# Two passes of cached attention and MLP on one core: rows 0 to 4 finished in mid-run, rows 5 to 7 together at the end, and wo loaded in longer runs

## The chip, the cores and the metric

One core of a Trainium2 chip. The time is what the device takes for one execution, in microseconds (us), as the median over several runs. Before the change it is 1152.2 us. (A trace is one execution. On the packet ruler below, the two traces of the run a_quick drift apart by up to 1.5 us.)

## The reference

Two blocks, A (attention with a cache) and B (an MLP with a mixer), are applied twice in turn to eight rows of one token each.

```python
# B = 8 rows, 1 token, D = 448; 16 query heads on 8 K/V heads, 4096 positions, Dh = 256
def _A_ref(x, k_cache, v_cache, wq, wo):
    q = (x @ wq) ...                        # 8 x 16 heads x 256
    scores = einsum("bhqd,bhkd->bhqk", q, k) * (Dh ** -0.5)
    o = einsum("bhqk,bhkd->bhqd", softmax(scores), v)
    return o.reshape(B, 1, 4096) @ wo
def _B_ref(x, w1, w2, w3, w4):
    ...                                     # the mixer shifts along a sequence of length 1: x1 = x
    return x1 + gelu(layernorm(x1) @ w3) @ w4
x = x + A(layernorm(x)); x = x + B(layernorm(x))
x = x + A(layernorm(x)); x = x + B(layernorm(x))
```

K and V are 128 MB each, in bf16. Both passes read all of them. A row has 32 MB of K and V, and the kernel's pool holds 15 MB of it at one time.

## The kernel before

K and V come in blocks of 1 MB into a pool of 15 slots. An item of the program is one block, K or V, of one row in one pass. Row b's second pass follows soon after its first, so ten blocks of each row are kept on the chip between the passes. Those ten slots are taken from the first pass of a row until its second one; the other five are all that the stream of blocks has in the meantime. I call these five the ring. Slots go back to the ring in the order in which they come free, and every load is issued from one queue (SyncE).

```python
NC = 15
kept = [(GP - 1, kv, n) for n in range(4) for kv in range(2)] + [(GP - 2, 0, n) for n in (0, 2)]
...
def emit_loads(most=None):
    while loads and places and n != most:
        it = loads.pop(0)
        p = where[it] = places.pop(0)
        ...
        nc.sync.dma_start(dst[:], src)          # 1 MB, in packets of 8192 B
```

A K block is transposed in place by VectorE, multiplied by TensorE and then free; a V block is multiplied by TensorE and then free. Between the items the program slips in steps of the per-row work (generators): the row's output projection, its MLP, and q of the second pass. After the second pass there is the *finish*: output projection, MLP and store. The kernel before finishes rows 0 to 6 together, under the last row's items, and the last row alone at the very end.

```python
def rest(b, st):                                # the finish of rows 0 .. 6
    nb = Bn - 1
    yield from out_cols(lambda i: OT2[:, i % 2, i // 2, :nb], wo_sb, NB2, 0, nb, 1)
    yield from mlp(0, nb)
    ...                                         # transpose, cast to bf16
    nc.sync.dma_start(out[:nb].rearrange("b s d -> (b s) d"), xo)
...
elif done == 4 and not final:
    add_gen("last", b, last(b, st), idx + 1, idx + (7 if b == Bn - 2 else 13), 6)
    if b == Bn - 2:
        add_gen("last", 0, rest(b, st), idx + 1, len(items) - 2, 21)
if not (ps == 0 and stays(it)):                 # the item's slot is free
    if final and stays(it) and at_end is not None:
        ...                                     # two slots become scratch for the end
    else:
        places.append(p)
emit_loads()
step(idx)
```

The last row's second-pass V blocks are used as the stationary operand, so that its output comes out in columns:

```python
def pv_cols(o_ps, v, a, gp):
    for y in range(16):
        for j in range(2):
            nc.tensor.matmul(o_ps[:, j, 2 * g : 2 * g + 2],
                v[:, y * Dh + 128 * j : y * Dh + 128 * j + 128],
                ptw[:, a, 4 * (y % 4) + y // 4, 6:8], ...)
...
nc.sync.dma_start(wo_sb[:], A_wo.rearrange("(g p) d -> p g d", p=128))
```

The softmax here doesn't subtract the row's maximum and nothing guards it: scores larger than these inputs give would overflow.

Of the kernel before, what the change touches and what calls it, by code (L numbers as in the profile page):

```python
# [17 lines left out]
def kernel(  # L18
# [43 lines left out]

    kept = [(GP - 1, kv, n) for n in range(4) for kv in range(2)] + [(GP - 2, 0, n) for n in (0, 2)]
    LAG = 4

    consts = ctx.enter_context(tc.tile_pool(name="consts", bufs=1))
    work = ctx.enter_context(tc.tile_pool(name="work", bufs=2))
# [119 lines left out]
    def norm(x, nb, twice):  # L187



        def room(name, shape, at):
            n = shape[0] * shape[1]
            if nb == 1:
                t = chn.tile([128, n], FP32, tag=name)
                ap = t[:]
            else:
                ap = scratch(at, n * nb)
            return ap.rearrange("p (s f b) -> p s f b", s=shape[0], f=shape[1])

        def bc(ap):  # L200
            return ap.unsqueeze(1).to_broadcast([128, 4, nb])

        xx = room("xx", (2, 4), 0)
        nc.vector.tensor_mul(xx[:, 0], x, wv[:].unsqueeze(2).to_broadcast([128, 4, nb]))
        nc.vector.tensor_mul(xx[:, 1], xx[:, 0], x)
        xs = room("xs", (1, 2), 512)[:, 0]
        nc.vector.tensor_reduce(
            xs, xx.rearrange("p s f b -> p s b f"), mybir.AxisListType.X, ALU.add
        )
        yield  # L210
        st = ps_m.tile([128, 2, nb], FP32, tag=bank[0])
        nc.tensor.matmul(st[:], ones, xs, start=True, stop=True)
        yield
        mv = room("mv", (1, 2), 528)[:, 0]
        nc.vector.tensor_copy(mv, st[:])
        var = room("var", (1, 1), 608)[:, 0, 0]
        if nb == 1:
            nc.vector.scalar_tensor_tensor(
                var, mv[:, 0], mv[:, 0], mv[:, 1], ALU.mult, ALU.subtract, reverse1=True
            )  # L220
        else:
            nc.vector.tensor_mul(var, mv[:, 0], mv[:, 0])
            nc.vector.tensor_sub(var, mv[:, 1], var)


        ve = room("ve", (1, 2), 544)[:, 0]
        n = 2 if twice else 1
        nc.vector.tensor_scalar(ve[:, 0], var, 0.0, EPS, ALU.max, ALU.add)
        if twice:
            nc.vector.tensor_scalar(ve[:, 1], var, 0.0, EPS * EPS / (1 + EPS), ALU.max, ALU.add)  # L230
        rs = room("rs", (1, 2), 560)[:, 0]
        nc.gpsimd.tensor_tensor(  # L232
            rs[:, 0:n].rearrange("p n b -> p (n b)"),
            ve[:, 0:n].rearrange("p n b -> p (n b)"),
            nhalf[:].to_broadcast([128, n * nb]),
            ALU.pow,
        )
        xc = room("xc", (1, 4), 576)[:, 0]
        nc.vector.tensor_tensor(xc, x, bc(mv[:, 0]), ALU.subtract)
        yield  # L240
        if nb > 1:
            yield
        c = (1 + EPS) ** -0.5 if twice else 1.0
        rl = rs[:, n - 1]
        parts = ((slice(0, 128), 0, 3, 0), (slice(0, 64), 3, 4, 3), (slice(64, 128), 3, 4, 4))
        for pp, f0, f1, to in parts:
            dst = xbs(nb)[pp, to : to + f1 - f0, :]
            if nb == 1:
                nc.vector.tensor_scalar(dst, xc[pp, f0:f1], rl[pp], c, ALU.mult, ALU.mult)
            else:  # L250
                nc.vector.scalar_tensor_tensor(
                    dst,
                    xc[pp, f0:f1],
                    c,
                    rl[pp].unsqueeze(1).to_broadcast([pp.stop - pp.start, f1 - f0, nb]),
                    ALU.mult,
                    ALU.mult,
                )
        if twice and nb == 1:
            nc.vector.scalar_tensor_tensor(x, xc, rs[:, 0], x, ALU.mult, ALU.add)  # L260
        elif twice:
            nc.vector.tensor_tensor(xc, xc, bc(rs[:, 0]), ALU.mult)
            nc.vector.tensor_add(x, x, xc)
        yield
# [130 lines left out]
    def half(o_ps, zall, g8, OT):  # L395


        rz = yield from z_cols(zall, range(2 * g8, 2 * g8 + 2))

        R = chn.tile([128, 8], FP32, tag="R")  # L400
        nc.vector.tensor_mul(
            R[:].rearrange("p (g n) -> p g n", n=4),
            rz[:].rearrange("p n g -> p g n"),
            fold[:].rearrange("p (g n) -> p g n", n=4),
        )
        o_sb = chn.tile([128, Dh], FP32, tag="o_sb")
        nc.scalar.copy(o_sb[:], o_ps[:, Dh * g8 : Dh * g8 + Dh])
        yield
        ot_ps = ot_bank[:, 64 * g8 : 64 * g8 + 16].rearrange("p (j h) -> p j h", j=2)
        for j in range(2):  # L410
            nc.tensor.matmul(  # L411
                ot_ps[:, j], o_sb[:, 128 * j : 128 * j + 128], R[:], start=True, stop=True
            )
        yield
        nc.vector.tensor_copy(OT[:, :, 8 * g8 : 8 * g8 + 8], ot_ps)
        yield
# [35 lines left out]
    def first_last(b, st):  # L452

        yield from half(st["o"], st["z"], 1, OT2[:, :, :, b])
        if b == Bn - 1:
            yield from add_half(st["y"], OT2[:, :, :, b : b + 1], 1, 1, claim(st), 2)

    def claim(st):

        return st.setdefault("begun", 0) == 0 and st.update(begun=1) is None  # L460
# [3 lines left out]

    def rest(b, st):

        nb = Bn - 1
        yield from out_cols(lambda i: OT2[:, i % 2, i // 2, :nb], wo_sb, NB2, 0, nb, 1)
        yield from mlp(0, nb)
        xh = scratch(768, 2 * nb).bitcast(BF16).rearrange("p (c b) -> p c b", c=4)  # L470
# [132 lines left out]
    def pv_cols(o_ps, v, a, gp):  # L603

        g = 2 * gp + a // 2
        for y in range(16):
            for j in range(2):
                nc.tensor.matmul(  # L608
                    o_ps[:, j, 2 * g : 2 * g + 2],
                    v[:, y * Dh + 128 * j : y * Dh + 128 * j + 128],  # L610
                    ptw[:, a, 4 * (y % 4) + y // 4, 6:8],
                    start=(a % 2 == 0 and y == 0 and j == 0),
                    stop=(a % 2 == 1 and y == 15),
                    skip_group_check=True,
                )
# [6 lines left out]
    ps0 = rows_to_cols(x_row, Bn)  # L622
    nc.vector.tensor_copy(xT[:], ps0[:])
    emit_loads(5)
    nc.sync.dma_start(wo_sb[:], A_wo.rearrange("(g p) d -> p g d", p=128))
    load_split(w3_sb, B_w3, F)
    nc.sync.dma_start(w4_sb[:], B_w4.rearrange("(c p) d -> p c d", p=128))
    for _ in project_q(0, Bn, qT1[:]):
# [13 lines left out]

    def step(idx):

        for kind in ("chain", "last"):
            bank[0] = kind
            e = next((e for e in gens if e["kind"] == kind), None)
            if e is None:
# [8 lines left out]
    first_of = {}  # L657
    for idx, (n, kv, c) in enumerate(items):
        first_of.setdefault((tasks[n][:2], kv), idx)
    yF, rz_gp, at_end = None, None, False  # L660

    for idx, it in enumerate(items):
        n, kv, c = it
# [4 lines left out]
        if kv == 0:  # L668
# [11 lines left out]
            if "o" not in st:  # L680
# [1 line left out]
                st["o"], st["z"] = o_banks[0], z_t  # L682
                o_banks.append(o_banks.pop(0))
                if final:
                    st["y"] = o_banks[0][:, 0:4].unsqueeze(2)
                    oc = st["o"][:, 0 : 2 * Hq].rearrange("p (j h) -> p j h", j=2)
            if not (ps == 1 and stays(it)):
                transpose_k(slot)
# [8 lines left out]
        else:  # L697
# [6 lines left out]
            if final and gp in free:  # L704
                pv_cols(oc, slot, c, gp)
                if c % 2 == 1:
# [4 lines left out]
                    run(  # L711
                        add_cols(
                            st["y"],
                            lambda i: OT2[:, i % 2, i // 2, b : b + 1],
                            wo_sb,
                            range(h0, h0 + 4),
                            1,
                            5,
                            first=claim(st),
                            stop=(gp == free[-1] and u == 1),  # L720
# [5 lines left out]
            if c == 3:  # L726
# [5 lines left out]
                elif done == 4 and ps == 0:  # L732
                    add_gen("chain", b, chain(b, st), idx + 1, first_of[(1, b), 0] - 1, 30)
                elif done == 4 and not final:
                    add_gen("last", b, last(b, st), idx + 1, idx + (7 if b == Bn - 2 else 13), 6)
                    if b == Bn - 2:
                        add_gen("last", 0, rest(b, st), idx + 1, len(items) - 2, 21)
        if not (ps == 0 and stays(it)):
            if final and stays(it) and at_end is not None:

                if not at_end:
                    at_end, spare[:] = True, []
                spare.append(slot)
                if len(spare) == 2:
                    at_end = None
            else:
                places.append(p)
        emit_loads()
        step(idx)
    while gens:  # L750
        step(10 * len(items))
    bank[0] = "last"


    xs = xT[:, :, Bn - 1 : Bn]
    nc.vector.tensor_add(xs, xs, st["y"])
    ident2 = spare[1][:, 0:256].bitcast(FP32)
    nc.vector.tensor_copy(ident2, identb[:])
    W = D // 4
    o_row = ps_m.tile([128, W], FP32, tag="chain")  # L760
    nc.vector.memset(o_row[:], 0.0)
    HT = run(mlp_hidden(Bn - 1, 1))
    for q in range(4):
        for fc in range(4):
            w = 128 if fc < 3 else 64
            lo, hi = max(W * q, 128 * fc), min(W * q + W, 128 * fc + w)
            if lo < hi:
                nc.tensor.matmul(
                    o_row[32 * q : 32 * q + 1, lo - W * q : hi - W * q],
                    xT[:w, fc, Bn - 1 : Bn],  # L770
                    ident2[:w, lo - 128 * fc : hi - 128 * fc],
                    start=(lo == W * q),
                    stop=False,
# [2 lines left out]
    for c in range(HC):  # L776
        for q in range(4):
            nc.tensor.matmul(
                o_row[32 * q : 32 * q + 1, :],
                HT[:, c, :],  # L780
                w4_sb[:, c, W * q : W * q + W],
                start=False,
# [2 lines left out]
            )  # L785
    xo = spare[1][:, 256 : 256 + W]
    nc.vector.tensor_copy(xo, o_row[:])
    nc.sync.dma_start(
        out[Bn - 1].rearrange("s (q w) -> (s q) w", q=4),
        xo.rearrange("(q r) w -> q r w", r=32)[:, 0, :],  # L790
    )


# [28 lines left out]
```

## Time and profile before

| before | us |
|---|---|
| median of the runs | 1152.2 |
| span of the profiled run | 1149.58 |
| 5,000th packet of 8192 B down | 123.53 |
| 44,000th / 48,000th packet of 8192 B down | 896.64 / 977.66 |
| last packet of 8192 B down (all K and V is on the chip) | 1131.96 |
| last matmul on V ends | 1137.82 |

The packet times are counted from the packet records in the trace, data packets of 8192 B in the order of their ends: wq's large pieces and all K and V blocks consist of such packets, 55,680 in each kernel that keeps ten blocks. They are a ruler along the run: the same packet number means the same bytes moved.

The page cuts the span into 40 slices. These are its rows for the granted TensorE clock, the busy share of the DMA engines and the rate, and its packet count:

```profile
PEclk9999998555755557555665557555575556555655
DMA  9999999999999999999999999999999999999993
GB/s 353 375 421 420 419 398 414 420 421 396 418 421 420 420 419 419 420 402 413 419 419 420 405 417 419 420 420 399 419 420 420 410 399 414 420 419 393 412 420 143
DMA packets 69500, 465.91 MB, mean 405 GB/s; under 512 B 7127, under 2 KB 13158, under 8 KB 13670
```

The DMA engines are the bound: busy in every slice but the last, at 420 GB/s in most. What is not at 420 is lost: the first two slices, in which the weights load, one dip in each row's cycle (398, 396, 402, 405, 399, 399, 393), and the tail.

The windows view gives for a stretch its length, the busy time and instruction count of each engine, the granted clock, the DMA share and GB/s. Here are the two stretches of before in which wo loads:

```profile
core 0: us, PE busy (x) PEld busy (x) DVE busy (x) ACT busy (x) POOL busy (x), PEclk, DMA share, GB/s
25.00:30.00 5.00, 2.05 (x64) 1.66 (x64) 4.97 (x3) 1.10 (x2) 0.00 (x0) 1.00 1.06 337
30.00:35.00 5.00, 1.24 (x36) 1.00 (x36) 0.00 (x0) 0.48 (x3) 0.00 (x0) 1.00 1.09 338
```

The engines are busy all the time (share over 1) and move only 337 GB/s: wo's rows come in packets of 896 B, which take 46 ns each at the median where one of 8192 B takes 312 (packet records of before). And the same view over the end of row 5's cycle, when row 6's ten kept blocks hold their slots and five are left:

```profile
905.00:920.00 15.00, 8.00 (x198) 6.58 (x199) 8.09 (x11) 1.87 (x4) 0.00 (x0) 0.50 1.00 400
920.00:935.00 15.00, 10.79 (x268) 8.50 (x268) 9.54 (x20) 1.49 (x3) 0.70 (x1) 0.50 1.00 391
935.00:950.00 15.00, 11.48 (x304) 9.23 (x297) 7.96 (x15) 0.27 (x1) 0.55 (x1) 0.50 1.00 407
950.00:965.00 15.00, 10.29 (x314) 8.02 (x313) 3.93 (x7) 3.48 (x7) 0.00 (x0) 0.68 1.01 410
```

I call this the tight stretch. Counted from the issue times and the packet records, 1.0 to 2.2 MB are outstanding there when the next load has been issued (bytes of all loads issued before it, less the bytes of packets that have ended).

The chain of waits of before (start, duration, what) near the end of the run, in extracts:

```profile
1087.62 1.80 PE y_ps L318 x64
...
1094.61 1.80 PE y_ps L318 x32
...
1103.78 2.60 POOL slot_80 L232
...
1107.30 2.22 DVE slot_86 L546
...
1120.03 1.21 PE y_ps L318 x28
...
1136.02 1.81 PE o_111 L608 x64
```

The chain there is TensorE's, not the DMA's. `y_ps` is the seven-row finish (output projection, later w4); the POOL piece is its pow over 14 columns, behind which VectorE and then a K transpose wait. The timeline (start, duration, engine, line, what, and in brackets the idle time before it) shows the last V blocks of before and what follows:

```profile
1133.94 1.01 PE L608 MATMUL o_111<-ptw,slot_79 128*128 128x2 bf16 x32
1135.95 1.01 PE L608 MATMUL o_111<-ptw,slot_88 128*128 128x2 bf16 x32
1136.83 0.99 PE L608 MATMUL o_111<-ptw,slot_82 128*128 128x2 bf16 x32
...
1146.75 0.27 DVE L787 CAST slot_87<-o_row 128x112 bf16<-128x112 f32 x1 [1.58 <-PE o_row L778]
1147.06 0.61 SPq L788 DMA_DIRECT2D out_dram<-slot_87  x1
```

The last bytes were down at 1131.96 us, yet TensorE comes to the last block only at 1136.83: it lags.

### The profile page before, as it was taken

How to read it: one execution, taken by the hardware profiler on the slowest of the kernel's cores; microseconds unless marked ns; L12 is line 12 of the kernel's file. 1: busy time of each engine (PE TensorE's matmuls, PEld its weight loads, DVE VectorE, ACT ScalarE, POOL GpSimd, SP SyncE). 2: the span in 40 equal slices, each digit the busy share in tenths (PEclk: the TensorE clock that was granted, in tenths of full speed). 3: DMA queues.
4: the chain of work that ended last, by engine and by line, in shares of the span. 5: the costliest groups of instructions: out<-in, count | busy, mean ns of one | idle time of the engine just before them, and what ended most of it. 6: DMA issues, size and time to landing. Idle time of an engine off the chain costs nothing. (4 is left out here: it accounts for less than half of the span.)

```text
span 1149.6 us, 36516 instructions
## 1 busy us (share of the span) xinstructions
PE 677.8 (59%) x17177; PEld 522.2 (45%) x17177; DVE 554.0 (48%) x712; ACT 114.1 (10%) x234; POOL 15.6 (1%) x25
## 2 busy tenths in 40 slices
PE   3134677557645665456754576536765476547786
PEld 2023455345533554345543455425544365426666
DVE  5145454455444545455354554445544554445452
ACT  0001011100110111001110101010011001010100
POOL 0000000000000000000000000000000000000000
PEclk9999998555755557555665557555575556555655
DMA  9999999999999999999999999999999999999993
GB/s 353 375 421 420 419 398 414 420 421 396 418 421 420 420 419 419 420 402 413 419 419 420 405 417 419 420 420 399 419 420 420 410 399 414 420 419 393 412 420 143
DMA packets 69500, 465.91 MB, mean 405 GB/s; under 512 B 7127, under 2 KB 13158, under 8 KB 13670
## 3 DMA queue, kind: packets, MB, share of 16 engines
q1 hardware_dynamic: 69350, 463.58, 98.5%
q8 instruction: 134, 2.20, 0.8%
q14 instruction: 16, 0.13, 0.0%
HBM read 463.54 MB, written 0.01 MB: 403 GB/s over the span
## 5 line engine op out<-in xcount | busy, mean ns | idle before, releaser
L553 PEld LDWEIGHTS <-qbd 128*8 128x8 bf16 x8192 | 200.5, 111 | 439.7 <-issue 340.5
L594 PEld LDWEIGHTS <-ptw 128*8 128x8 bf16 x3968 | 110.2, 111 | 78.0 <-issue 29.4
L562 ACT ACTIVATE p_n<-sc_110 128x512 bf16<-128x512 f32 x32 | 42.5, 1327 | 409.0 <-PE sc_110 L553 409.0
L562 ACT ACTIVATE p_n<-sc_109 128x512 bf16<-128x512 f32 x32 | 42.5, 1327 | 382.3 <-PE sc_109 L553 382.3
L318 PEld LDWEIGHTS <-wo_sb 128*128 128x128 bf16 (+1 forms) x1600 | 64.4, 124 | 16.1 <-issue 15.3
L546 DVE STREAM_TRANSPOSE slot_79<-slot_79 128x2048 uint32<-128x2048 uint32 x19 | 43.8, 2308 | 39.0 <-DMA slot_79<-in_A_k_cache_dram 36.0
L546 DVE STREAM_TRANSPOSE slot_86<-slot_86 128x2048 uint32<-128x2048 uint32 x19 | 43.9, 2311 | 38.6 <-DMA slot_86<-in_A_k_cache_dram 36.0
L546 DVE STREAM_TRANSPOSE slot_81<-slot_81 128x2048 uint32<-128x2048 uint32 x18 | 41.6, 2309 | 37.4 <-DMA slot_81<-in_A_k_cache_dram 37.4
L318 PE MATMUL y_ps<-OT,wo_sb 128*128 128x1 bf16 (+1 forms) x1280 | 55.1, 176 | 3.0 <-issue 3.0
L546 DVE STREAM_TRANSPOSE slot_89<-slot_89 128x2048 uint32<-128x2048 uint32 x16 | 37.0, 2310 | 32.1 <-DMA slot_89<-in_A_k_cache_dram 32.0
L546 DVE STREAM_TRANSPOSE slot_88<-slot_88 128x2048 uint32<-128x2048 uint32 x15 | 34.6, 2308 | 29.8 <-DMA slot_88<-in_A_k_cache_dram 29.8
L546 DVE STREAM_TRANSPOSE slot_90<-slot_90 128x2048 uint32<-128x2048 uint32 x14 | 32.3, 2308 | 31.9 <-DMA slot_90<-in_A_k_cache_dram 31.9
L546 DVE STREAM_TRANSPOSE slot_82<-slot_82 128x2048 uint32<-128x2048 uint32 x14 | 32.3, 2307 | 29.5 <-DMA slot_82<-in_A_k_cache_dram 29.5
L546 DVE STREAM_TRANSPOSE slot_80<-slot_80 128x2048 uint32<-128x2048 uint32 x14 | 32.3, 2304 | 29.3 <-DMA slot_80<-in_A_k_cache_dram 29.3
L546 DVE STREAM_TRANSPOSE slot_84<-slot_84 128x2048 uint32<-128x2048 uint32 x12 | 27.7, 2309 | 37.5 <-DMA slot_84<-in_A_k_cache_dram 37.3
L546 DVE STREAM_TRANSPOSE slot_78<-slot_78 128x2048 uint32<-128x2048 uint32 x13 | 30.0, 2310 | 29.4 <-DMA slot_78<-in_A_k_cache_dram 29.4
L274 PEld LDWEIGHTS <-wq_sb 128*128 128x128 bf16 x1152 | 33.9, 104 | 18.2 <-issue 16.6
L546 DVE STREAM_TRANSPOSE slot_83<-slot_83 128x2048 uint32<-128x2048 uint32 x13 | 30.0, 2306 | 25.2 <-DMA slot_83<-in_A_k_cache_dram 25.2
L546 DVE STREAM_TRANSPOSE slot_92<-slot_92 128x2048 uint32<-128x2048 uint32 x12 | 27.6, 2304 | 21.8 <-DMA slot_92<-in_A_k_cache_dram 21.8
L582 ACT CAST ptw<-misc 128x128 bf16<-128x128 f32 x64 | 17.5, 273 | 203.9 <-PE misc L575 160.1
L274 PE MATMUL q_ps<-xb_126,wq_sb 128*128 128x1 bf16 x1024 | 31.8, 165 | 4.0 <-issue 2.7
L546 DVE STREAM_TRANSPOSE slot_87<-slot_87 128x2048 uint32<-128x2048 uint32 x10 | 23.1, 2311 | 20.6 <-DMA slot_87<-in_A_k_cache_dram 20.5
(217 smaller groups left out, 958.1 us busy)
## 6 DMA issues: line engine op xcount, KB each, us to landing
slot_79<-in_A_k_cache_dram SPq DMA_DIRECT2D x19, 1024.0 KB, 14.8
slot_86<-in_A_k_cache_dram SPq DMA_DIRECT2D x19, 1024.0 KB, 19.1
slot_81<-in_A_v_cache_dram SPq DMA_DIRECT2D x19, 1024.0 KB, 18.9
slot_81<-in_A_k_cache_dram SPq DMA_DIRECT2D x18, 1024.0 KB, 12.6
slot_89<-in_A_v_cache_dram SPq DMA_DIRECT2D x17, 1024.0 KB, 9.7
slot_82<-in_A_v_cache_dram SPq DMA_DIRECT2D x17, 1024.0 KB, 17.6
slot_86<-in_A_v_cache_dram SPq DMA_DIRECT2D x17, 1024.0 KB, 10.2
slot_88<-in_A_v_cache_dram SPq DMA_DIRECT2D x17, 1024.0 KB, 13.6
```

The source lines that it names most:

```text
L274: nc.tensor.matmul(q_ps[:, j * Hq + h, :], w, xbs(nb)[:, xi, :], start=(fc == 0), stop=(fc == 3),)
L318: nc.tensor.matmul(r, w[:, i, lo:hi], rhs(i), start=(first and fc == 0 and i == rows[0]), stop=(stop and i == rows[-1]), skip_group_check= ...
L546: nc.vector.transpose(w, w)
L553: nc.tensor.matmul(sc[32 * k : 32 * k + 8, 128 * x : 128 * x + 128], qbd[:, ep, gp].rearrange("p a h -> p (a h)"), kv[:, k, 2 * half + e2, ...
L562: nc.scalar.activation(p_sb[:].rearrange("p t i x -> p x t i"), sc[:].rearrange("p (x t i) -> p x t i", x=4, t=4), ACT.Exp, scale=scale_ex ...
L582: nc.scalar.copy(ptw[:, :, :, 6:8], pt_ps.rearrange("p t k (a h) -> p a (t k) h", a=4),)
L594: nc.tensor.matmul(o_ps[32 * q : 32 * q + 8, 256 * (g // 4) : 256 * (g // 4) + 256], ptw[:, a, 4 * (y % 4) + y // 4, w : w + 8], v[:, y * ...
```

## The change

Three things are meant. The finish of most rows leaves the end of the run, where it delays the last row, and goes to mid-run, where the engines beside the DMA have time (over the span of before PE is busy for 59% and VectorE for 48%). The last three rows share one finish, since their row count hardly changes the number of matmuls (for one row at the end of before 160 on wo and 56 on w3). And wo's rows are laid so that a partition holds d = 2p and 2p+1 of each head, which makes one run of 1792 B out of two of 896 B; for this V and o_sb are read with a step of two as stationary operands. The diff also splits the pow of the layernorm, one instruction for each of its variances, the one that is needed first in front. The finish in mid-run needs scratch space, and takes a slot of the ring for it until it is done. The diff, cut to its core:

```diff
+    R = Bn - 3
@@ norm
-        nc.gpsimd.tensor_tensor(rs[:, 0:n] ..., ve[:, 0:n] ..., nhalf ..., ALU.pow)
+        for i in range(n)[::-1]:
+            nc.gpsimd.tensor_tensor(rs[:, i], ve[:, i], nhalf[:].to_broadcast([128, nb]), ALU.pow)
@@ half
-                ot_ps[:, j], o_sb[:, 128 * j : 128 * j + 128], R[:], start=True, stop=True
+                ot_ps[:, j], o_sb[:, j : Dh : 2], Rz[:], start=True, stop=True
@@ first_last (the last row)
-            yield from add_half(st["y"], OT2[:, :, :, b : b + 1], 1, 1, claim(st), 2)
+            yield from add_half(st["y"], OT2[:, :, :, R:], 1, Bn - R, claim(st), 2)
@@ rest
-        nb = Bn - 1
+        nb = R
@@ pv_cols
-                    v[:, y * Dh + 128 * j : y * Dh + 128 * j + 128],
+                    v[:, y * Dh + j : y * Dh + Dh : 2],
@@ loads
-    nc.sync.dma_start(wo_sb[:], A_wo.rearrange("(g p) d -> p g d", p=128))
+    nc.sync.dma_start(
+        wo_sb[:].rearrange("p (h j) d -> p h j d", j=2),
+        A_wo.rearrange("(h p j) d -> p h j d", p=128, j=2),
+    )
@@ the item loop
-                    add_gen("last", b, last(b, st), idx + 1, idx + (7 if b == Bn - 2 else 13), 6)
-                    if b == Bn - 2:
-                        add_gen("last", 0, rest(b, st), idx + 1, len(items) - 2, 21)
+                    add_gen("last", b, last(b, st), idx + 1, idx + 13, 6)
+                    if b == R - 1:
+                        rest_from = idx + 14
...
+            elif borrow == "wanted":
+                borrow, spare[0] = p, slot
             else:
                 places.append(p)
+        if type(borrow) is int and not any(e["kind"] == "rest" for e in gens):
+            places.append(borrow)
+            borrow = None
         emit_loads()
+        if idx == rest_from:
+            borrow = "wanted"
+            add_gen("rest", 0, rest(b, st), idx + 4, idx + 60, 22)
@@ the end
-    xs = xT[:, :, Bn - 1 : Bn]
+    xs = xT[:, :, R:]
...                                             # the same with three columns
-    nc.sync.dma_start(out[Bn - 1] ...)
+    for n in range(nb):
+        (nc.sync, nc.scalar)[n % 2].dma_start(out[R + n] ...)
```

More of the change, by code (lines that the diff above doesn't have):

```diff
@@ L231, in norm @@
         rs = room("rs", (1, 2), 560)[:, 0]
-        nc.gpsimd.tensor_tensor(
-            rs[:, 0:n].rearrange("p n b -> p (n b)"),
-            ve[:, 0:n].rearrange("p n b -> p (n b)"),
-            nhalf[:].to_broadcast([128, n * nb]),
-            ALU.pow,
-        )
+        for i in range(n)[::-1]:
+            nc.gpsimd.tensor_tensor(rs[:, i], ve[:, i], nhalf[:].to_broadcast([128, nb]), ALU.pow)
         xc = room("xc", (1, 4), 576)[:, 0]
@@ L240, in norm @@
         yield
-        if nb > 1:
+        if nb > 3:
             yield
@@ L398, in half @@
         rz = yield from z_cols(zall, range(2 * g8, 2 * g8 + 2))
-        R = chn.tile([128, 8], FP32, tag="R")
+        Rz = chn.tile([128, 8], FP32, tag="Rz")
         nc.vector.tensor_mul(
-            R[:].rearrange("p (g n) -> p g n", n=4),
+            Rz[:].rearrange("p (g n) -> p g n", n=4),
             rz[:].rearrange("p n g -> p g n"),
@@ L643, in step @@
     def step(idx):
-        for kind in ("chain", "last"):
+        for kind in ("chain", "last", "rest"):
             bank[0] = kind
@@ L659 @@
         first_of.setdefault((tasks[n][:2], kv), idx)
-    yF, rz_gp, at_end = None, None, False
+    rz_gp, rest_from, borrow, ends = None, None, None, []
     for idx, it in enumerate(items):
@@ L684 @@
                 if final:
-                    st["y"] = o_banks[0][:, 0:4].unsqueeze(2)
+                    st["y"] = o_banks[0][:, 0 : 4 * (Bn - R)].rearrange("p (f b) -> p f b", f=4)
                     oc = st["o"][:, 0 : 2 * Hq].rearrange("p (j h) -> p j h", j=2)
@@ L713 @@
                             st["y"],
-                            lambda i: OT2[:, i % 2, i // 2, b : b + 1],
+                            lambda i: OT2[:, i % 2, i // 2, R:],
                             wo_sb,
                             range(h0, h0 + 4),
-                            1,
+                            Bn - R,
                             5,
@@ L734 @@
                 elif done == 4 and not final:
-                    add_gen("last", b, last(b, st), idx + 1, idx + (7 if b == Bn - 2 else 13), 6)
-                    if b == Bn - 2:
-                        add_gen("last", 0, rest(b, st), idx + 1, len(items) - 2, 21)
+                    add_gen("last", b, last(b, st), idx + 1, idx + 13, 6)
+                    if b == R - 1:
+                        rest_from = idx + 14
         if not (ps == 0 and stays(it)):
-            if final and stays(it) and at_end is not None:
-                if not at_end:
-                    at_end, spare[:] = True, []
-                spare.append(slot)
-                if len(spare) == 2:
-                    at_end = None
+            if final and stays(it) and len(ends) < 2:
+                ends.append(slot)
+                if len(ends) == 2:
+                    spare[:] = ends
+            elif borrow == "wanted":
+                borrow, spare[0] = p, slot
             else:
                 places.append(p)
+        if type(borrow) is int and not any(e["kind"] == "rest" for e in gens):
+            places.append(borrow)
+            borrow = None
         emit_loads()
+        if idx == rest_from:
+            borrow = "wanted"
+            add_gen("rest", 0, rest(b, st), idx + 4, idx + 60, 22)
         step(idx)
@@ L751 @@
         step(10 * len(items))
-    bank[0] = "last"
-    xs = xT[:, :, Bn - 1 : Bn]
+    bank[0] = "rest"
+    nb = Bn - R
+    xs = xT[:, :, R:]
     nc.vector.tensor_add(xs, xs, st["y"])
@@ L761 @@
     nc.vector.memset(o_row[:], 0.0)
-    HT = run(mlp_hidden(Bn - 1, 1))
+    HT = run(mlp_hidden(R, nb))
     for q in range(4):
@@ L768 @@
                 nc.tensor.matmul(
-                    o_row[32 * q : 32 * q + 1, lo - W * q : hi - W * q],
-                    xT[:w, fc, Bn - 1 : Bn],
+                    o_row[32 * q : 32 * q + nb, lo - W * q : hi - W * q],
+                    xT[:w, fc, R:],
                     ident2[:w, lo - 128 * fc : hi - 128 * fc],
@@ L778 @@
             nc.tensor.matmul(
-                o_row[32 * q : 32 * q + 1, :],
+                o_row[32 * q : 32 * q + nb, :],
                 HT[:, c, :],
@@ L787 @@
     nc.vector.tensor_copy(xo, o_row[:])
-    nc.sync.dma_start(
-        out[Bn - 1].rearrange("s (q w) -> (s q) w", q=4),
-        xo.rearrange("(q r) w -> q r w", r=32)[:, 0, :],
-    )
+    for n in range(nb):
+        (nc.sync, nc.scalar)[n % 2].dma_start(
+            out[R + n].rearrange("s (q w) -> q (s w)", q=4),
+            xo.rearrange("(q r) w -> q r w", r=32)[:, n],
+        )
 _INS = ['A_x', 'A_k_cache', 'A_v_cache', 'A_wq', 'A_wo', 'B_x', 'B_w1', 'B_w2', 'B_w3', 'B_w4']
```

## The prediction

> **What bounds it now.** The DMA engines. The page's slice row shows DMA at 9 in all but the last slice, mostly 420 GB/s; 466 MB at that rate are about 1,109 of 1,149.6 us. By five-microsecond windows the rest is a 3 us start, about 5 us lost while weights load (337 GB/s between 25 and 35 us, with wo), some 12 us in dips to 360-390 GB/s late in each row's cycle, and a tail without DMA. In the timeline the last V block's bytes are down near 1,132 us, but it is used up only at 1,137.8; the last row's MLP and store end at 1,149.6.
>
> The tail lags because TensorE, at a granted clock near 0.5, is nearly the whole chain of waits from 1,087 us on. It holds the seven-row finish: out projection (160 matmuls, 4.6 us), w3 (1.8), w4 (2.9), transpose (0.5), and 2.6 us in which VectorE, and K transposes behind it, wait for GpSimd's 14-column pow.
>
> **Terms, estimates from those durations.**
>
> 1. wo in 1792 B runs. Its 4,096 packets of 896 B take 46 ns each (8192 B: 312; 3584 B: 144); a line through these gives 79 ns for 1792 B, the few in the trace took 88. [...] 11.8 us become 10.1 to 11.3; DMA-bound, so it counts: -1.2 us.
>
> 2. The seven-row finish leaves the tail. Without its 10 us of TensorE work and the pow wait, the last V block is done about 2 us after landing instead of 6: -3.7 us.
>
> 3. The three-row finish is wider. Matmul counts are equal; the first pow has 3 columns (one 0.55 us, two 0.70, so 0.85), variance takes one more VectorE instruction (0.2), gelu 42 columns, the third store follows the first on its queue (0.6): +1.1 us on the final chain.
>
> 4. The five-row finish borrows one of five free ring slots (ten of fifteen hold kept K/V) for some 50 items, just over row 5's tight stretch (908 to 957 us now). There 1.0 to 1.6 MB are outstanding before each issue, and a slot is held about 4 us after landing. With four slots, and the finish's own work, the DMA will sometimes run dry; today this stretch loses 2 us of 45, I expect 4 to 5. Lost DMA time is not regained: +2.3 us (0 to 6).
>
> 5. Stride-2 weight loads of V and o_sb: no cost. [...] the trace's stride-2 selector loads take about 26 ns apart, but none is 128 columns wide.
>
> Sum -1.5; I lean slightly lower. All 8192 B traffic stays, so 2% is very unlikely.
>
> **Predicted: 1150 us, range 1145 to 1155. Faster by over 2%: 0.02; within 2%: 0.96; slower: 0.02.**
>
> **What would show it.** 1: more GB/s from 25 to 37 us, the first V block used 1 us earlier. 2: no seven-column matmuls late; the last V block used within 2 us of landing. 3: from the last V matmul to the end about 13 us, now 11.8. 4: a deeper GB/s dip at 905 to 960 us with less outstanding, and in no other row. 5: 32 of the last row's V weight loads still in 0.95 us.
>
> **What would make it wrong.** Four slots starving the DMA much more (1153 and up) or not at all (1147); slower strided weight loads (up to 1 us per V block at the end); TensorE still lagging in the last row from instruction stalls; dearer output stores.

-1.2, -3.7, +1.1, +2.3 and nothing for term 5 make the -1.5. Term 5 rests on the selector loads alone (15 of them take 0.42 us at 171.86 us of before), and for loads of 128 columns it was my estimate. The instruction stalls and dearer stores named at its end are possibilities, not findings.

## The result and the profile after

After: 1152.53 us median (1151.27 to 1153.37, four runs); before beside it 1152.24. The ratio is 1.0002 with a 95% interval of 0.9984 to 1.0019: the same. (A ratio here is the mean time of one kernel's fast runs over that of the other's fast runs of the same rounds, so it is not quite the ratio of the medians.)

Nothing gained, but not because nothing happened. The traces on the common ruler:

| us | before | after | difference |
|---|---|---|---|
| 5,000th packet of 8192 B down | 123.53 | 122.51 | -1.02 |
| 44,000th | 896.64 | 895.57 | -1.07 |
| 44,000th to 48,000th (row 5's tight stretch) | 81.02 | 85.31 | +4.29 |
| 48,000th to the last | 154.30 | 154.82 | +0.52 |
| last packet to the end of the last matmul on V | 5.86 | 1.50 | -4.36 |
| from there to the end of the span | 11.76 | 12.80 | +1.04 |
| span | 1149.58 | 1150.00 | +0.42 |

From the page after, the rate by slices and the packets:

```profile
GB/s 356 387 421 418 421 397 419 420 419 397 419 419 420 417 419 420 420 401 413 419 419 420 407 415 419 421 419 399 420 419 419 391 372 397 420 421 395 400 420 191
DMA packets 67464, 465.91 MB, mean 405 GB/s; under 512 B 7141, under 2 KB 11122, under 8 KB 11634
```

The second slice rose from 375 to 387 (wo), and slices 32 to 34 fell from 410, 399, 414 to 391, 372, 397: the dip of one row's cycle is deeper, and of no other row by as much. Some 2,000 packets fewer are wo's. The windows view after, first where wo loads, then over the tight stretch:

```profile
25.00:30.00 5.00, 2.05 (x64) 1.66 (x64) 5.00 (x3) 0.94 (x1) 0.00 (x0) 1.00 1.02 374
30.00:35.00 5.00, 1.24 (x36) 1.00 (x36) 0.13 (x1) 0.64 (x3) 0.00 (x0) 1.00 1.06 384
...
905.00:920.00 15.00, 8.65 (x211) 7.14 (x211) 9.01 (x16) 1.92 (x5) 0.00 (x0) 0.50 0.92 364
920.00:935.00 15.00, 12.09 (x307) 9.88 (x310) 8.84 (x20) 1.49 (x3) 1.07 (x2) 0.50 0.98 373
935.00:950.00 15.00, 12.50 (x322) 10.30 (x315) 7.50 (x17) 0.27 (x1) 0.54 (x1) 0.50 0.97 367
```

337 became 374 and 384 GB/s. In the tight stretch 400, 391 and 407 became 364, 373 and 367, and the DMA share fell to 0.92: the engines ran out of work. By the same count as before, 0.4 to 1.5 MB are outstanding when a load is issued there, more often than not under 0.8. In before, just before the stretch, up to 890 us, it is nearly 6 MB.

The chain of waits after, from 1082 us on:

```profile
1082.23 14.22 DMA slot<-in_A_v_cache_dram
...
1096.53 19.75 DMA slot<-in_A_v_cache_dram
...
1116.36 19.78 DMA slot<-in_A_v_cache_dram
1136.14 0.05 issue
1136.19 1.03 PE o L605 x32
```

It is the DMA's now, to the last V block: TensorE waits for the bytes. The tail did what was hoped of it, and the bytes come 3.74 us later. The last V blocks and the stores in the timeline after:

```profile
1135.06 2.14 PE L605 MATMUL o<-ptw,slot 128*128 128x2 bf16 x64
1137.24 0.23 DVE L388 TENSOR_TENSOR qT<-o,rz 128x2 bf16<-128x2 f32 x2 [2.93 <-PE o L605]
...
1146.49 0.27 DVE L795 CAST slot<-o_row 128x112 bf16<-128x112 f32 x1 [1.58 <-PE o_row L786]
1146.80 1.18 SPq L797 DMA_DIRECT2D out_dram<-slot  x2
1146.84 1.39 ACTq L797 DMA_DIRECT2D out_dram<-slot  x1
```

From the end of the cast to the end of the span it takes 3.24 us, against 2.56 before (1149.58 less 1147.02); the chain from the last V matmul to that cast takes 9.56 us against 9.20.

### The profile page after: what moved, and what is told of

Read it like the earlier page. It is cut to its first block, busy times and chain, and to the rows that moved or that the text cites. A ratio compares the mean times of both kernels' runs of the same rounds, so it can differ in the third digit from the quotient of the medians.

```text
span 1150.0 us, 36534 instructions
## 1 busy us (share of the span) xinstructions
PE 673.3 (59%) x17177; PEld 518.6 (45%) x17177; DVE 554.1 (48%) x714; ACT 113.7 (10%) x234; POOL 19.1 (2%) x35
## 5 line engine op out<-in xcount | busy, mean ns | idle before, releaser
L543 DVE STREAM_TRANSPOSE slot<-slot 128x2048 uint32<-128x2048 uint32 x208 | 479.7, 2309 | 444.5 <-DMA slot<-in_A_k_cache_dram 440.8
L550 PE MATMUL sc<-slot,qbd 128*8 128x128 bf16 x8192 | 250.6, 289 | 394.2 <-DVE slot L543 280.1
L591 PE MATMUL o<-slot,ptw 128*8 128x256 bf16 x3968 | 241.2, 386 | 44.1 <-DMA slot<-in_A_v_cache_dram 25.2
L559 ACT ACTIVATE p_n<-sc 128x512 bf16<-128x512 f32 x64 | 84.5, 1321 | 797.0 <-PE sc L550 797.0
L271 PE MATMUL q_ps<-xb,wq_sb 128*128 128x1 bf16 (+1 forms) x1152 | 35.6, 166 | 11.3 <-DMA wq_sb<-in_A_wq_dram 3.7
L408 PEld LDWEIGHTS misc<-Rz,o_sb 128*128 128x128 f32 x124 | 26.1, 292 | 11.2 <-issue 11.2
L408 PE MATMUL misc<-Rz,o_sb 128*128 128x8 f32 x124 | 29.0, 344 | 0.0
L234 POOL TENSOR_TENSOR t<-t,nhalf 128x1 f32<-128x1 f32 x24 | 12.8, 544 | 976.9 <-DVE t L236 886.2
L315 PEld LDWEIGHTS <-w_sb 128*128 128x128 bf16 (+1 forms) x630 | 25.3, 124 | 6.9 <-issue 5.4
L315 PE MATMUL y_ps<-HT_t,w_sb 128*128 128x1 bf16 (+1 forms) x560 | 24.2, 177 | 0.3 <-DVE HT_t L356 0.3
L378 PE MATMUL misc<-zm,one 128*128 128x8 f32 (+1 forms) x66 | 18.3, 350 | 6.2 <-ACT ptw L579 6.2
```

The lines of the kernel that those rows point to most:

```text
L234: nc.gpsimd.tensor_tensor(rs[:, i], ve[:, i], nhalf[:].to_broadcast([128, nb]), ALU.pow)
L271: nc.tensor.matmul(q_ps[:, j * Hq + h, :], w, xbs(nb)[:, xi, :], start=(fc == 0), stop=(fc == 3),)
L315: nc.tensor.matmul(r, w[:, i, lo:hi], rhs(i), start=(first and fc == 0 and i == rows[0]), stop=(stop and i == rows[-1]), skip_group_check= ...
L378: nc.tensor.matmul(z_ps, ones, zm[:], start=True, stop=True)
L408: nc.tensor.matmul(ot_ps[:, j], o_sb[:, j : Dh : 2], Rz[:], start=True, stop=True)
L543: nc.vector.transpose(w, w)
```

## The experiments

The gain of the tail and of wo (5.4 us together) is paid back mainly in one stretch of 80 us. Two theories say why the DMA runs dry there.

- **S (slot):** the finish holds one of the five ring slots just through the tight stretch; with four, too little is outstanding.
- **W (work):** the finish's TensorE, VectorE and GpSimd work in that stretch delays the use of blocks, so that slots come free later. In the windows above TensorE is indeed busier after (12.09 and 12.50 us of 15 against 10.79 and 11.48).

All kernels ran five rounds. In the first four-kernel call before had a median of 1151.82 us, in the second 1151.72, in the third 1151.51. All gave correct results but b_no_finish. "Stretch" in what follows is the time from the 44,000th to the 48,000th packet of 8192 B, 81.02 us in before and 85.31 after; "lag" is the time from the last such packet to the end of the last V matmul.

### b_slot: the slot held, no finish in mid-run

```diff
 (before)
+            elif idx >= 370 and held is None:
+                held = p
             else:
                 places.append(p)
+        if idx == 422:
+            places.append(held)
         emit_loads()
```

> The kernel before, with the slot that the changed kernel borrows kept out of the ring for the same items (370 to 422), and nothing else: no finish in mid-run. Theory S (the missing slot starves the DMA): packets 44,000 to 48,000 take 4 us longer than in before (85 instead of 81.0), the rate between 910 and 950 us falls to about 350 to 375 GB/s, the run is 3.5 to 5 us longer. Theory W (the finish's TensorE and VectorE work holds slots longer): this kernel loses under 1 us against before.

Measured: 1155.04 us, ratio 1.003 (1.0017 to 1.0043), stretch 84.79 us. Its tight stretch in the windows view:

```profile
905.00:920.00 15.00, 7.50 (x180) 6.07 (x181) 8.10 (x11) 1.89 (x4) 0.00 (x0) 0.50 0.93 365
920.00:935.00 15.00, 10.67 (x258) 8.39 (x256) 9.39 (x20) 1.49 (x3) 0.70 (x1) 0.50 1.00 374
935.00:950.00 15.00, 11.32 (x316) 9.53 (x319) 6.75 (x16) 0.27 (x1) 0.55 (x1) 0.50 0.96 357
```

These are the rates of after (364, 373, 367) with TensorE no busier than in before. The slot alone makes 3.8 of the 4.3 us. W is left with half a microsecond at most, which is within what one trace differs from another (below).

The traces say more about that rest. From 905 to 960 us b_slot is no faster than after (371 against 374 GB/s), so no cost of the work shows there. The difference comes after it. Here are ten microseconds of after and then of b_slot, and what SyncE waited for before its next load (us in all, times, longest), in after and then in a_quick (the run below):

```profile
960.00:970.00 10.00, 5.33 (x210) 4.48 (x213) 4.35 (x4) 1.84 (x4) 0.00 (x0) 0.96 0.96 381
960.00:970.00 10.00, 4.81 (x166) 3.89 (x169) 3.82 (x4) 1.84 (x4) 0.00 (x0) 0.94 1.01 420
SPq L536 <- DMA out_dram<-slot: 6.0, 1, 6.0
SPq L536 <- DMA out_dram<-slot: 10.5, 1, 10.5
```

The finish ends with a store from the borrowed slot, issued at 956.04 us in after. The load that goes into this slot waits for the store to land, and every later load stands behind it in the one queue: 6.0 us without an issue, and 381 GB/s where before has 421, which is about 1 us. So giving the slot back costs time too; no run took this out by itself.

### a_quick: the finish over before the stretch begins

```diff
 (after)
-            add_gen("rest", 0, rest(b, st), idx + 4, idx + 60, 22)
+            add_gen("rest", 0, rest(b, st), idx + 4, idx + 30, 22)
```

> The changed kernel with the five-row finish spread over 26 items and not 56, so that it is over and the slot is back at about 890 us, ahead of the tight stretch. Theory S: packets 44,000 to 48,000 take about 81 us again, the last V block lands at 1,131 to 1,132, and the run is about 4 us shorter than the changed kernel and than before: near 1,148.3 (ratio to before about 0.9965). Theory W: the same work in half the time delays as much or more, and the run stays at 1,152 or above.

Measured: 1148.58 us, ratio to before 0.9971 (0.9958 to 0.9985), stretch 81.35 us, last packet at 1131.67, lag 1.51. Its windows:

```profile
905.00:920.00 15.00, 8.80 (x214) 7.27 (x214) 7.79 (x12) 1.87 (x4) 0.00 (x0) 0.50 0.99 397
920.00:935.00 15.00, 10.45 (x254) 7.82 (x252) 9.07 (x20) 1.49 (x3) 1.06 (x2) 0.50 0.99 392
935.00:950.00 15.00, 11.43 (x312) 9.45 (x312) 8.64 (x15) 0.27 (x1) 0.54 (x1) 0.50 1.00 401
```

The dip is that of before again. The same slot is taken and the same work is done, but while nearly 6 MB are outstanding. Three windows of this time, and one after the slot has come back:

```profile
860.00:870.00 10.00, 8.74 (x221) 6.43 (x217) 7.32 (x9) 0.28 (x1) 2.31 (x2) 0.50 1.01 415
870.00:880.00 10.00, 8.86 (x213) 7.10 (x217) 6.61 (x10) 1.94 (x5) 0.00 (x0) 0.50 1.01 421
880.00:890.00 10.00, 7.16 (x158) 5.42 (x147) 5.32 (x7) 1.31 (x2) 0.00 (x0) 0.60 1.01 419
900.00:910.00 10.00, 3.98 (x112) 3.06 (x112) 4.96 (x7) 1.33 (x2) 0.00 (x0) 0.50 1.00 406
```

TensorE is busy for 24.8 us of 30, and the rate stays at 415 to 421 GB/s, so neither the work nor the borrowing costs the DMA anything there. The return of the slot nearly does: the store, issued at 887.5 us behind all the loads outstanding, keeps SyncE from issuing for 10.5 us (second line of waits above), and what is outstanding falls from 4.9 to 1.4 MB by 900 us. The price is small, 406 GB/s where before has 420, some 0.3 us, but the slack was all but used up. One constant recovers what the change had lost.

### a_quick_again: does it repeat

The same kernel. It was run at another time.

> The quick version a second time, so that the two that follow can be held against it on one chip, and to see whether its gain repeats: near 1,148.6, ratio to before 0.997.

Measured: 1148.2 us, ratio 0.9971 (0.9955 to 0.9987); stretch 81.60 us, lag 1.47. It repeats.

### a_same: the changed kernel again

No edit.

> The changed kernel again, as it is, so that the others of this call can be held against it on one chip. All theories: within 0.2% of before, near 1,152.

Measured: 1152.53 us, ratio 1.0011 (0.9994 to 1.0027). Its profiled run was a long one (span 1154.4), with a stretch of 88.0 us where the first trace had 85.3. So the loss in the stretch is not one fixed number; 4 to 7 us were seen in two traces.

### b_slot2: two slots held

```diff
 (b_slot)
-            elif idx >= 370 and held is None:
-                held = p
+            elif idx >= 370 and len(held) < 2:
+                held.append(p)
...
-            places.append(held)
+            places.extend(held)
```

> The kernel before with two slots kept out of the ring for items 370 to 422, so three are left where one slot less left four. Theory S: the loss grows faster than in proportion, since nothing is outstanding any more when a slot comes free: packets 44,000 to 48,000 take 95 to 105 us (five slots 81.0, four 84.8), the run is 15 to 25 us longer than before. If the first slot's 3.8 us had another cause, such as the order of slots, about 3 to 8 us longer.

Measured: 1160.55 us, ratio 1.008 (1.0063 to 1.0097), stretch 88.04 us. My number was far off: the second slot cost 3.2 us in the stretch, no more than the first (3.8), where I had expected 10 to 20. In a window from 905 to 960 us the rate is 400 GB/s with five slots (before), 371 with four (b_slot) and 346 with three. A ring of three still moved most of the bytes. By the packet records a load between 910 and 950 us lands at the median 6.6 us after its issue with five slots, 6.0 with four and 4.9 with three, so each slot is held for a shorter time; whether its block is also used sooner after landing was not counted. By its own numbers (8.8 us longer by the medians) this run fell far short of what I had given to theory S, 15 to 25 us, and just above the 3 to 8 us given to "another cause". Both ranges rested on an expected steepness which turned out wrong, and the run does not decide between the theories. b_slot and a_quick do.

### b_keep9: six slots in every row's stretch

```diff
 (before)
-    kept = [...] + [(GP - 2, 0, n) for n in (0, 2)]
+    kept = [...] + [(GP - 2, 0, n) for n in (0,)]
```

> The kernel before with nine kept blocks instead of ten, so that six slots are free in the tight stretch of every row; one more block of 1 MB is read for each row, 8 in all, which at 2.49 us each is 19.9 us of DMA. If the dips at the end of each row's cycle come from too few free slots, they nearly vanish and give back some 6 to 10 us, and the run is 10 to 14 us longer. If the dips come from something else, such as TensorE and VectorE work at the row's end, the run is 18 to 20 us longer.

Measured: 1167.29 us, ratio 1.0132 (1.0116 to 1.0149), 15.6 us longer by the medians. Between the two: of 19.9 us of added loads (an estimate, 8 MB at the 421 GB/s measured) 4.3 us came back. On the ruler the 55,680th packet is down at 1127.31 us, 4.65 us ahead of before. But the split isn't clean: in this trace the last packet of all comes at 1150.62 us, 18.7 us later than in before, and 3.0 of the 4.3 us lie in a shorter lag (2.82 us against 5.86). So the dips that every row has anyway are in part a matter of free slots, but over eight rows at most some 4 us of them; with six slots the rate still falls to 380 to 406 GB/s late in row 5's cycle (930 to 970 us in this run). What makes the rest of them stays open.

### b_no_finish: what the seven-row finish costs in the tail

```diff
 (before; rows 0 to 6 are never written, wrong on purpose)
-                    if b == Bn - 2:
-                        add_gen("last", 0, rest(b, st), idx + 1, len(items) - 2, 21)
```

> The kernel before without the seven-row finish; rows 0 to 6 are left unwritten, so the result is wrong on purpose. It shows what that finish costs in the tail. If its TensorE work and pow wait are what holds the last V blocks back, the time from the last 8192 B packet to the last V matmul falls from 5.9 to about 1.5 us, the last packet comes at the same 1,132 us, and the run is 4 to 4.5 us shorter: near 1,147.9. If the tail lags for another reason (throttled clock, instruction stalls), under 1.5 us shorter.

Measured: 1147.83 us, ratio 0.9968 (0.9955 to 0.9981), lag 1.48 us. Its last V block in the timeline:

```profile
1135.09 1.01 PE L608 MATMUL o<-ptw,slot 128*128 128x2 bf16 x32 [1.25 <-DMA slot<-in_A_v_cache_dram]
```

TensorE now waits for the block. (In this trace the last packet came at 1134.62 and not at 1132, as its DMA had run some 2.5 us behind from the first half on; the lag does not depend on that.) The lag fell by 4.4 us and the run by 4.0 us by the medians when the finish was taken out. How much of a lag the finish makes differs from trace to trace, though: in the other kernels that keep it in the tail the lag is 5.56 us (b_slot), 5.52 (b_slot2), 3.24 (b_wo) and 2.82 (b_keep9). Without it, it was 1.5 us each time.

### b_wo: the layout of wo alone

```diff
 (before)
-    nc.sync.dma_start(wo_sb[:], A_wo.rearrange("(g p) d -> p g d", p=128))
+    nc.sync.dma_start(wo_sb[:].rearrange("p (h j) d -> p h j d", j=2),
+                      A_wo.rearrange("(h p j) d -> p h j d", p=128, j=2))
... and the two stride-2 reads of V and o_sb, as in the change
```

> The kernel before with nothing changed but wo's layout (and the two stride-2 weight loads that go with it). The changed kernel's trace is 1.0 us ahead of before at the 5,000th packet of 8192 B. If the layout is a plain gain of DMA time, the whole run is 0.8 to 1.3 us shorter (ratio about 0.999), the lead is 1 us at the 5,000th, the 44,000th and the last packet, and the time from the last such packet to the last V matmul stays 5.9 us. If the lead is eaten by the end (the tail is set by TensorE and not by the last byte), the run is the same to 0.3 us. If stride-2 loads of V cost, the 32 loads of a V block take longer than 0.95 us.

Measured: 1150.22 us, ratio 0.999 (0.9974 to 1.0005). The time alone does not decide. The trace does for the start: the 5,000th packet is down at 122.18 us, 1.35 us ahead of before, and the 44,000th 0.99 us ahead. In this one trace the lead was still 1.3 us at the 54,656th packet and gone at the last (1132.09), while the last V matmul ended 2.5 us earlier than in before: the lag was 3.24 us and not the 5.9 that I had expected to stay. Here TensorE and not the last byte sets the tail, so the time of the last byte says little. Nor is the lead always kept: a_quick_again and a_quick_st have it at the 5,000th packet (0.96 and 0.82 us) and at the 20,000th no more than a quarter of a microsecond of it, so the drift between traces is as large as this gain.

### a_quick_r6: six rows in mid-run, two at the end

```diff
 (a_quick)
-    R = Bn - 3
+    R = Bn - 2
```

> The changed kernel with the finish spread over 26 items and with rows 0 to 5 in it, rows 6 and 7 at the end. The finish then comes after row 5's last block, about 1,060 us on, with row 6's tight stretch still open when the slot is taken. If two rows at the end are cheaper than three (one store less, 0.6 us, and a narrower chain, 0.2 us) and the borrowed slot does no harm there, about 0.8 us shorter than the quick version at 1,148.6. If theory S holds and the slot is taken within the tight stretch, or the finish again delays the last V blocks, 1 to 4 us longer than the quick version. I expect the second, near 1,150.

Measured: 1150.85 us, ratio 0.9988 (0.9973 to 1.0004), 2.3 us above a_quick by the medians. It was run at another time. The end of the span comes 12.28 us after the last V matmul (12.8 with three rows, 11.76 with one), but the lag is 4.91 us: the finish is again under the last row's items, and TensorE lags again. It is not the DMA this time: the last packet came at 1131.33.

### a_quick_st: the third store from GpSimd

```diff
 (a_quick)
-        (nc.sync, nc.scalar)[n % 2].dma_start(
+        (nc.sync, nc.scalar, nc.gpsimd)[n % 3].dma_start(
```

> The quick version with the third output row's store issued by GpSimd, not as the second of the SyncE queue. From the cast of the last result to the end of the span the changed kernel took 3.24 us and before 2.56. If the second issue on one queue (0.6 us) is the reason, this falls to about 2.6 us; if the slowest of the three is ScalarE's store (issue 1.39 us), it stays at 3.2; if GpSimd's store is dearer, 3.5 to 4.5. In the run's time none of these can be told from noise of 0.15%.

Measured: 1148.07 us, ratio 0.9965 (0.995 to 0.998). From the cast to the end 3.50 us, against 3.24 in a_quick_again. Moving the third store did not help. It does not follow that the second issue on SyncE's queue cost nothing, for the traces have the landings too. Counted from the end of the cast, a_quick_again's stores land at 1.67 us (SyncE's first), 2.03 (ScalarE's) and 2.31 (SyncE's second), and the one store of before at 1.67. So there the second issue does set the last landing, 0.64 us later than one store would. In a_quick_st that landing is gone, but ScalarE's comes at 2.18 and GpSimd's at 2.03, and from the last landing to the end of the span it takes 1.32 us, where the other traces have 0.9. Why the end is longer there stays open.

### a_quick_w4: the same idea carried on to w4

w4 is laid so that a partition holds seven successive hidden units, which makes runs of 6272 B; w3's weight loads then step by seven elements.

```diff
 (a_quick)
-    nc.sync.dma_start(w4_sb[:], B_w4.rearrange("(c p) d -> p c d", p=128))
+    nc.sync.dma_start(
+        w4_sb[:].rearrange("p (u c) d -> p u (c d)", u=2),
+        B_w4.rearrange("(u p c) d -> p u (c d)", u=2, p=128),
+    )
...
-                w, xi = wblk(w3_sb, F, c, fc)
+                u, k = c // (HC // 2), c % (HC // 2)
+                xi = fc if fc < 3 else 3 + u
+                o = fc * F + (u * F // 2 if fc < 3 else 0) + k
+                w = w3_sb[:, o : o + F // 2 - k : HC // 2]
```

> The quick version with w4 laid like wo, but further: hidden unit 7p+c of each half on partition p, so that w4 loads in 6272 B runs (256 packets and not 1,792) and w3's weight loads step by 7 elements. At 49 ns a packet of 896 B, 5.5 us of engine time become about 3.9: 1.5 us less DMA time, the first V block used at about 47.5 us and not 49.1. If a step of 7 costs nothing in the weight load, the run is 1.5 us shorter than the quick version, near 1,147, and the 56 w3 matmuls of the last chain still take 1.65 us. If it slows the load, those 56 take 2 us or more and the run gains less or nothing.

Measured: 1152.36 us, ratio 1.0006 (0.9991 to 1.0022): about 4 us *longer* than a_quick_again beside it. The load did gain: the 5,000th packet is down at 121.20 us against 122.57, the first V block used at 47.91 and not 49.11. But the weight load with a step of seven is dear: 154 ns at the median over the run, against 104 in a_quick_again. The 56 matmuls on w3 in the last chain, in the timeline of a_quick_again and then of a_quick_w4:

```profile
1138.09 1.64 PE L333 MATMUL h_ps<-xb,w_sb 128*128 128x3 bf16 x56 [2.12 <-DVE xb L248]
```

```profile
1143.14 3.10 PE L336 MATMUL h_ps<-xb,w_sb 128*128 128x3 bf16 x56 [2.12 <-DVE xb L248]
```

The last chain is 1.5 us longer for it (14.28 against 12.81 us after the last V matmul). The same loads occur in every row's MLP, and in the groups view the time that these matmuls keep TensorE busy rises from 18.0 to 32.7 us over the run. The last packet of 8192 B came at 1136.74 us, 5 us later than in a_quick_again: between 905 and 960 us the rate is 388 GB/s against 400, between 1060 and 1110 us 394 against 411. I take it that TensorE's added work delays the release of slots, that is, theory W at work where five slots are just enough. This is argued and not shown: no run separates it. The profiled run was the longest of its six (1154.68 us); by the medians the kernel is 4.2 us longer, of which the last chain makes 1.5 and the loads about 2.7.

## Why the prediction was right, and where it was not

The time was in the range (1145 to 1155, measured 1152.5), and so was the class, but the range was wide: I predicted 1150, a gain of about 2 us, and there was none. The sum of the terms was -1.5 us where the traces have +0.4. Term by term:

1. **wo in longer runs: -1.2 us predicted, -1.0 in the trace of after, -1.35 in b_wo.** Right at the 5,000th packet, and for the reason given: wo's packets take 78 ns for 1792 B where two of 896 B took 92. So a longer packet is cheaper than two of half its size, by 15%; why it is, is not shown. By these medians 16 engines move about 312 GB/s in packets of 896 B, 368 of 1792 B and 420 of 8192 B (311 to 312 ns), an estimate.
2. **The seven-row finish leaves the tail: -3.7 predicted, -4.36 measured** as lag. b_no_finish shows the cause by itself: lag 1.48 us without it. The size holds for this pair of traces; with the finish in the tail lags from 2.8 to 5.9 us were seen. a_quick_r6 shows it the other way round: a finish brought back under the last row's items brings the lag back.
3. **The wider last chain: +1.1 predicted, +1.04 measured.** The parts were a little different: 0.36 for the chain and 0.68 for the stores, where I had 0.5 and 0.6. The first pow with three columns took 0.86 us (0.85 expected); in these two traces one column took 0.54, two 0.70, five 1.17 and fourteen 2.59. That the third store comes 0.6 us late because it is second on its queue is what the landings show (0.64 us); but a_quick_st shows that moving it to another queue does not win this back.
4. **The borrowed slot: +2.3 predicted (0 to 6), +4.3 measured.** This is the term that was mis-sized; net it is the whole miss, since the smaller differences of the other terms cancel. The mechanism was right: b_slot makes 3.8 us of it without any of the finish's work, and a_quick takes it away by giving the slot back earlier. What the term left out is the store at the finish's end, behind which the queue stands for 6.0 us. I expected the stretch to lose 4 to 5 us in all where it loses 2 in before; with one slot less it loses about 6. Nor was the lost time regained after it: from the 48,000th packet to the last it took 154.82 us, against 154.30.
5. **Stride-2 weight loads: no cost predicted, none measured.** V's loads take 104 ns each at the median before and after, and 32 of them about 1 us. o_sb is fp32; its loads take 331 ns at the median after and 333 before, so the step costs nothing there either. This holds for a step of two: with a step of seven a_quick_w4's loads on w3 take 154 ns at the median instead of 104.

What I had not seen in the prediction is that the loss was avoidable: the slack before the tight stretch, with nearly 6 MB outstanding, was in the numbers that I had. The finish fits in there, and a_quick beats both kernels: it is at 0.9971 of before (at most 0.9987), where the changed kernel is at 1.0002 and 1.0011 (at least 0.9984 and 0.9994). The twelve runs of a_quick (1146.9 to 1150.1 us) all lie below the ten of the changed kernel (1151.3 to 1156.5). The gain is 0.3%.

## What to carry to other kernels

Where the DMA is the bound, as here, a buffer of the load ring can be part of the DMA's speed (from 905 to 960 us 400 GB/s with five slots, 371 with four and 346 with three): ask of every change that takes a buffer not only how long it holds it but *when*, and look at the bytes outstanding at each issue in that stretch (here nearly 6 MB went with 420 GB/s, 1.0 to 2.2 MB with about 400, and 0.4 to 1.5 MB with 364 to 373). Ask too what the buffer's return waits for: here a store that had to land first held up every load behind it in the queue, for 6.0 us in after and 10.5 in a_quick. Work that is moved off the end of a run can lose its gain elsewhere; put both kernels on one ruler (the same number of bytes moved), so that a null result splits into the gains and the loss that make it up. And longer runs for a small weight were worth about a microsecond here (wo, 1.0 and 1.35 us at the 5,000th packet), and that only where the compute side read the new layout at its old speed: w4's gained 1.37 us there, and the kernel became 4.2 us longer.
